# Scores of stage A as 64-row matmul pairs from one unpadded copy of the keys

## The chip, the cores and the metric

The kernel runs on one core of a Trainium2 chip. The metric is device time of one execution in microseconds (us), the median over several runs. The core has five engines that run side by side and meet at semaphores: PE (TensorE: matmuls, with weight loads, PEld, beside them), DVE (VectorE), ACT (ScalarE), POOL (GpSimd) and SP (SyncE, which here only issues DMAs). Each engine takes its own instructions strictly in the order in which the program has them, so an instruction that waits holds up all that stand behind it on that engine.

## What is computed

Two stages over 8 batches. Stage A is attention with a soft cap (12 heads, 448 tokens, 64 features per head); its output, with the heads put side by side as 768 features, is the input of stage B, a mixture of four attention experts with a causal mask and a top-2 gate.

```python
scores = scale * np.matmul(q, k.transpose(0, 1, 3, 2))
scores = cap * np.tanh(scores / cap)
attn = np.exp(scores)            # over the sum of its row
attn_out = np.matmul(attn, v)
...
x = attn_out, heads side by side
logits = x @ w_gate              # top 2 of 4 experts, softmax over the two
for e in range(E):
    q, k, v = x @ wq[e], x @ wk[e], x @ wv[e]
    a = causal softmax(scale * (q @ k.transpose(0, 2, 1)))
    out += gate[e] * (a @ v @ wo[e])
```

## The kernel before

Stage A works on pairs of heads, p = 0 to 47, six pairs to a batch. The loop over `prog` is the order of ACT: for each pair four tanh instructions `("T", p, 0..3)` and two exponentials `("E", p, 0..1)`, and, in two pairs of each batch, two exponentials of stage B, `("X", b, r, g)`, for the batch before. Each T or X reads a score tile in PSUM of 2 x 512 columns; there are two such tiles (`ps_score`, bufs=2), so the matmuls that fill one for the n-th read (`fill`, `b_fill`) can start when the read n-2 is over.

The path of one pair. SP loads q, k and v of two pairs at a time (`load`). POOL casts them to f16 (`a_cast`): q (L241), k (L242), the last 64 keys of both heads as two blocks on the diagonal of a 128x128 tile `ktz` (L245), then v. PE transposes q, `ktz` and k into one PSUM tile `tps` (`a_tr`, L272, L277, L279), and DVE copies that to SBUF: queries `qt` (L289, L293), the block-diagonal tail keys `kt` (L296) and the main keys, each head by itself, to `kk = kz[p % 4]` (L295, L297; the copies show as L223, the line of the helper `evac`). In `qt` the two heads lie one above the other, 64 rows each. In `kz` each head has its own columns, with zeros in the rows of the other head, so that a matmul over all 128 rows gives the scores of one head. `HALF` says which (head, block of 128 keys) are in each of the four score tiles: seven matmuls of 128 rows by 448 columns for a pair (L312), of which the tail block serves both heads at once. After tanh (L323) and exponential (L330), `a_pv_mm` multiplies with v (L351) and with the tail of v (`vtz`, L346), `a_pv_out` divides by the sums on DVE, and `a_xt` transposes the result into `xT` (L379, L390).

Stage B of a batch follows while stage A of the next batch runs. For each pair r of experts it has the projections q and k (`b_qk`, six matmuls each, L469), v and the gate's logits (`b_v`, L407), scores (`b_fill`, L522, L528), exponential (L540), a causal mask by POOL (L548), `b_pv` (L570), `b_ot` and `b_wo` (L594), copies to `ob` by DVE (L223), and the stores. Its weights are loaded by POOL, which issues up to three DMAs of the list `loads` in each `slot(p)` (L746), behind the casts of that slot.

What sets the order of PE: a planner, `Plan`, run in Python when the kernel is built. It keeps clocks of PE, DVE and ACT, and a list of work units with a PE time, a DVE time, dependences and a due time. Before each fill `do_fill` lets the planner put in as many units as fit ahead of the time at which ACT will need the fill (`plan.pump(rel, at - cost - 0.4)`), where `cost` is the PE time that the fill is taken to need. So a number in `do_fill` decides where the units of stage B stand between the fills. The planner takes no account of the DMAs of the weights: the first units of stage B depend on `x` (the transposed output of stage A) alone. At the end `last_batch` does stage B of batch 7 by itself; the units of batch 6 that are left by then are put in between.

```python
cost = 0.43 if o[0] == "X" else 0.38 if o[2] < 3 else 0.19
...
plan.pump(rel, at - cost - 0.4)
...
plan.parts(("q", b, r), 3, 1.13, 0.55, [x], t - 4.0, b_qk, b, r, "q")
```

Of the kernel before, what the change touches and what calls it, by code (L numbers as in the profile page):

```python
# [8 lines left out]
f32 = mybir.dt.float32  # L9
# [116 lines left out]
def kernel(  # L126
# [87 lines left out]
    nc.vector.memset(warm, 0.0)  # L214
    ident = const.tile([128, 128], f16, name="ident")
    make_identity(nc, ident)
    kz = [const.tile([128, 2, KM], f16, name=f"kz{i}") for i in range(4)]
    ktz = [const.tile([128, 128], f16, name=f"ktz{i}") for i in range(6)]
    for t in (ktz[0], kz[0], ktz[1], kz[1]):
        nc.vector.memset(t, 0.0)  # L220

    def evac(dst, src, act=False):
        (nc.scalar.copy if act else nc.vector.tensor_copy)(dst, src)  # L223
# [5 lines left out]
    def a_cast(p, eng=None):  # L229
        if p >= NP:  # L230
            return
        eng = nc.gpsimd if eng is None else eng
        if 2 <= p < len(ktz):
            nc.gpsimd.memset(ktz[p], 0.0)
        if 2 <= p < len(kz):
            nc.gpsimd.memset(kz[p], 0.0)
        assert p < 8 or ("pv", p - 8, 1) in plan.done and ("tr", p - 6) in plan.done
        qf, kf, vf, ktf, vtf = staged.pop(p)
        q16 = hd.tile([QP, QC, 2, Dh], f16, name=f"q16_{p}", tag="q16", bufs=6)
        k16 = hd.tile([128, KC, 2, Dh], f16, name=f"k16_{p}", tag="k16", bufs=6)  # L240
        eng.tensor_copy(q16, qf.rearrange("p h (c d) -> p c h d", c=QC))  # L241
        nc.gpsimd.tensor_copy(k16, kf.rearrange("p h (c d) -> p c h d", c=KC))  # L242
        for g in range(2):
            r = slice(64 * g, 64 * (g + 1))
            eng.tensor_copy(ktz[p % 6][r, r], ktf[r, :])  # L245
        cast[p] = (q16, k16)
        vcast[p] = (vf, vtf)
        if p > 1:
            a_castv(p)
# [16 lines left out]

    def a_tr(p):
        q16, k16 = cast.pop(p)
        assert p < 4 or (p - 4) not in qkt
        tps = ps_aux.tile([128, 1024], f16, name=f"tps_{p}", tag="aux")  # L270
        for c in range(QC):
            nc.tensor.transpose(  # L272
                tps[:, c * QP : (c + 1) * QP],
                q16[:, c, :, :].rearrange("p h d -> p (h d)"),
                ident[0:QP, 0:QP],
            )
        nc.tensor.transpose(tps[:, S : S + 128], ktz[p % 6], ident)  # L277
        for c in range(KC):
            nc.tensor.transpose(  # L279
                tps[:, S + 128 * (c + 1) : S + 128 * (c + 2)],  # L280
                k16[:, c, :, :].rearrange("p h d -> p (h d)"),
                ident,
            )


        qt = hd.tile([128, S], f16, name=f"qt_{p}", tag="qt", bufs=4)
        kt = hd.tile([128, 128], f16, name=f"kt_{p}", tag="kt", bufs=4)
        m = tps[:, 0:S].rearrange("m (c p) -> m c p", c=QC)
        nc.vector.tensor_copy(  # L289
            qt[:, 0:KM].rearrange("m (n c t) -> m n c t", n=3, c=QC),  # L290
            m[:, :, 0:96].rearrange("m c (n t) -> m n c t", t=32),
        )
        nc.vector.tensor_copy(qt[:, KM:S].rearrange("m (c t) -> m c t", c=QC), m[:, :, 96:QP])  # L293
        kk = kz[p % 4]
        evac(kk[0:64, 0, :], tps[0:64, S + 128 : S + 512], act=(p == 0))  # L295
        nc.vector.tensor_copy(kt, tps[:, S : S + 128])  # L296
        evac(kk[64:128, 1, :], tps[64:128, S + 128 : S + 512], act=(p == 0))  # L297
        qkt[p] = (qt, kk, kt)

    HALF = (((0, 0), (0, 1)), ((0, 2), (0, 3)), ((1, 0), (1, 1)), ((1, 2),))
    score = {}

    def fill(p, i):
        qt, kk, kt = qkt[p]
        if i == 3:
            del qkt[p]
        sc = ps_score.tile([128, 2, 512], f32, name=f"s{i}_{p}", tag="score")
        for o, (g, c) in enumerate(HALF[i]):  # L310
            lhsT = kt if c == KC else kk[:, g, 128 * c : 128 * (c + 1)]
            nc.tensor.matmul(sc[:, o, 0:S], lhsT, qt, start=True, stop=True)  # L312
        score[(p, i)] = sc

    y = {}
# [1 line left out]

    def tanh(p, i):
        g = i // 2
        n = len(HALF[i])  # L320
        if i % 2 == 0:
            y[(p, g)] = actp.tile([128, 4 - g, S], f16, name=f"y{g}_{p}", tag=f"y{g}")
        nc.scalar.activation(  # L323
            y[(p, g)][:, 2 * (i % 2) : 2 * (i % 2) + n, :], score.pop((p, i))[:, 0:n, 0:S],
            AF.Tanh, scale=isc / capf,
        )
# [7 lines left out]

    pvs = {}

    def a_pv_mm(p, i, n, heads):

        if n == 0 and 0 in heads:
            pvs[p, i] = ps_aux.tile([128, 2, 2, Dh + 1], f32, name=f"pv{i}_{p}", tag="aux")  # L340
        pv = pvs[p, i]
        w = WIN[2 * i + n]
        for g in heads:
            pt = pr[(p, g)]
            if g == 0:
                nc.tensor.matmul(  # L346
                    pv[:, n, :, :], pt[:, KC, w : w + 128], vtz[p % 8], start=(n == 0),
                    stop=False, skip_group_check=True,
                )
            for c in range(KC):  # L350
                nc.tensor.matmul(  # L351
                    pv[:, n, g, :], pt[:, c, w : w + 128], v16[p % 8][:, g, c, :],
                    start=False, stop=(c == KC - 1), skip_group_check=True,
                )

    def a_pv_out(p, i):
        pv = pvs.pop((p, i))
# [312 lines left out]
    def rows(w):  # L670
        return w.rearrange("(c p) m -> p c m", p=128)

    loads = [(wvg[:, :, E * Dh : E * Dh + E], rows(moe_w_gate))]
    for r in range(2):
        for e in (2 * r, 2 * r + 1):
            cols = slice(e % 2 * Dh, (e % 2 + 1) * Dh)
            loads += [(wq2[r][:, :, cols], rows(moe_wq[e])), (wk2[r][:, :, cols], rows(moe_wk[e]))]
        if r == 0:
            for e in range(E):
                loads += [(wvg[:, :, e * Dh : (e + 1) * Dh], rows(moe_wv[e]))]  # L680
    for e in range(E):
        loads += [(wo2[e // 2][e % 2 * Dh : (e % 2 + 1) * Dh, :], moe_wo[e])]


    EXPB = {HP * (b + 1) + 3 + 2 * r - (b == B - 2) * r: (b, r) for b in range(B - 1) for r in range(2)}
# [18 lines left out]
    def dur(o):  # L704
        if o[0] == "S":
            return 0.0
        if o[0] == "X":
            return 0.9
        return 0.06 + 0.373 * (4 - o[2] if o[0] == "E" else len(HALF[o[2]]))

    def fill_dep(o):
        return (("tr", o[1]),) if o[0] == "T" else (("q", o[1], o[2]), ("k", o[1], o[2]))
# [1 line left out]
    def do_fill():  # L714
        nonlocal nfill
        o = reads[nfill]
        rel = ends[nfill - 2] if nfill >= 2 else 0.0
        cost = 0.43 if o[0] == "X" else 0.38 if o[2] < 3 else 0.19
        for d in fill_dep(o):
            plan.force(d)  # L720
        at = plan.act + sum(dur(x) for x in prog[pos : where[nfill]])
        plan.pump(rel, at - cost - 0.4)
        plan.pe = max(plan.pe, rel, *(plan.done[d] for d in fill_dep(o))) + cost
        fill(*o[1:]) if o[0] == "T" else b_fill(*o[1:])
        plan.done[("f", nfill)] = plan.pe + plan.LAT
        nfill += 1
# [10 lines left out]
    def slot(p):  # L737
# [5 lines left out]
            plan.done[("cast", p + CAST)] = plan.act + 4.0  # L743
        for _ in range(3 if p else 1):
            if loads:
                nc.gpsimd.dma_start(*loads.pop(0))  # L746
        if p in (4, 5):
            b_const(p - 4)
        for i in (1, 2) if p == 0 else (p + TR,):
# [23 lines left out]
    def batch(b):  # L773
        x = ("xt", HP * b + HP - 1)
        t0, t1 = nom["X", b, 0, 0], nom["X", b, 1, 0]
        pace = 1.0 if b < B - 2 else 0.3
        for r, t in enumerate((t0, t1)):
            plan.parts(("q", b, r), 3, 1.13, 0.55, [x], t - 4.0, b_qk, b, r, "q")
            plan.parts(("k", b, r), 3, 1.13, 0.75, [x], t - 4.0, b_qk, b, r, "k")
        for n in range(4):  # L780
            d = [("v", b, n - 1)] if n else [x]
            plan.parts(("v", b, n), 2, 0.66, 0.6, d, t0 + 2.0 * n, b_v, b, n)
        plan.add(("g1", b), 0.0, 1.0, [("v", b, 3)], t1 + 1.0, b_gate, b, aux=None)
        plan.add(("g", b), 0.0, 0.8, [("g1", b), ("G", b)], t1 + 3.0, b_gate2, b, aux=None)
        for e in range(E):
            due = t1 + pace * (6.0 + 3.0 * e)
            d = [("X", b, e // 2, e % 2), ("g", b)] + [("pvB", b, e - 1)] * (e % 2)
            plan.add(("pvB", b, e), 0.46, 0.7, d, due, b_pv, b, e)
            if e % 2:
                plan.add(("oT", b, e // 2), 0.22, 0.35, [("pvB", b, e)], due, b_ot, b, e // 2)  # L790
        for n in range(4):
            for f in range(2):
                i = 2 * n + f
                d = [("oT", b, 1)] if i == 0 else [("wo", b, *divmod(i - 1, 2))]
                due = t1 + pace * (19.0 + 1.5 * i)
                plan.add(("wo", b, n, f), 0.33, 0.5, d, due, b_wo, b, n, f)

# [173 lines left out]
```

## Time and profile before

| what | us |
|---|---|
| median of 5 runs (339.12 to 341.41) | 340.76 |
| the profiled execution, its own time | 341.25 |
| its span, first to last instruction | 339.5 |
| ACT busy, 341 instructions | 308.4 |
| PE busy | 283.1 |
| DVE busy | 250.9 |
| POOL busy | 164.3 |
| tanh (L323), 192 instructions | 152.9 |
| exponential of stage A (L330), 96 instructions | 150.1 |
| score matmuls of stage A (L312), 336 instructions | 100.3 |

The span runs from the first to the last instruction; the time of an execution is 1.75 us longer. Busy times of several engines overlap. A matmul's record holds its way through the array too, so that records of matmuls that follow closely overlap: a lone matmul of 448 columns shows 0.35 us, while such matmuls in a row start every 0.19 us. The mean granted clock of TensorE is 0.975 of full speed. In a timeline each row has the start, the time to the end of the group, the engine, line and operation, the tiles (out<-in), the sizes, the number of instructions merged into the row, and in square brackets the idle time before it and what ended that.

### The profile page before, as it was taken

How to read it: one execution, taken by the hardware profiler on the slowest of the kernel's cores; microseconds unless marked ns; L12 is line 12 of the kernel's file. 1: busy time of each engine (PE TensorE's matmuls, PEld its weight loads, DVE VectorE, ACT ScalarE, POOL GpSimd, SP SyncE). 2: the span in 40 equal slices, each digit the busy share in tenths (PEclk: the TensorE clock that was granted, in tenths of full speed). 3: DMA queues.
4: the chain of work that ended last, by engine and by line, in shares of the span. 5: the costliest groups of instructions: out<-in, count | busy, mean ns of one | idle time of the engine just before them, and what ended most of it. 6: DMA issues, size and time to landing. Idle time of an engine off the chain costs nothing.

```text
span 339.5 us, 8954 instructions
## 1 busy us (share of the span) xinstructions
PE 283.1 (83%) x3295; PEld 192.1 (57%) x3295; DVE 250.9 (74%) x877; ACT 308.4 (91%) x341; POOL 164.3 (48%) x527
## 2 busy tenths in 40 slices
PE   4777668988899789997999779997999879979762
PEld 1354445655566556765676556765576657666441
DVE  2356646688668996789786997789796997787582
ACT  2989999999999999999999999999999999993612
POOL 2789999738507490538416580629325610220220
PEclk9779999999999999999999999999999999999797
DMA  6999999900354706590259307570441002110116
GB/s 160 266 311 248 261 248 238 249 2 3 128 173 126 227 4 215 163 274 4 82 177 287 110 2 235 181 238 2 138 151 42 3 2 93 48 26 2 46 58 223
DMA packets 65148, 46.21 MB, mean 136 GB/s; under 512 B 25872, under 2 KB 61584, under 8 KB 65104
## 3 DMA queue, kind: packets, MB, share of 16 engines
q1 hardware_dynamic: 53712, 43.43, 43.4%
q0 software_dynamic: 10512, 1.58, 6.5%
q10 hardware_dynamic: 880, 0.62, 0.7%
q8 instruction: 26, 0.43, 0.5%
q14 instruction: 18, 0.15, 0.1%
HBM read 36.19 MB, written 11.01 MB: 139 GB/s over the span
## 4 chain that ended last, share of the span: by engine, by line
ACT 82%; PE 4%; DMA 4%; POOL 3%; DVE 2%; issue 2%; SPq 1%; POOLq 0%; DVEq 0%
ACT y L323 38%; ACT p L330 36%; ACT pB L540 7%; DMA kf<-in_k_dram 1%; DMA ktf<-in_k_dram 1%; POOL pB L548 1%; PE qkps L469 1%; DMA out_dram<-ob 1%; PE vps L407 1%; DVE ob L223 1%; PE sB L528 1%; SPq L188 1%; PE pv L351 0%; POOL ktz L245 0%; PE wops L594 0%
## 5 line engine op out<-in xcount | busy, mean ns | idle before, releaser
L323 ACT ACTIVATE y<-s 128x896 f16<-128x896 f32 x192 | 152.9, 884 | 1.8 <-PE s L312 1.8
L330 ACT ACTIVATE p<-y 128x1792 f16<-128x1792 f16 x96 | 150.1, 1567 | 0.0
L548 POOL TENSOR_SCALAR_AFFINE_SELECT pB<-pB 128x128 f16<-128x128 f16 (+1 forms) x128 | 31.7, 277 | 140.7 <-ACT pB L540 139.6
L312 PE MATMUL s<-qt,kz 128*128 128x448 f16 x288 | 83.2, 361 | 14.8 <-ACT y L323 6.9
L351 PE MATMUL pv<-v,p 128*128 128x65 f16 x1152 | 66.7, 195 | 0.5 <-ACT p L330 0.3
L351 PEld LDWEIGHTS <-p 128*128 128x128 f16 x1152 | 54.4, 99 | 10.3 <-ACT p L330 1.2
L346 PE MATMUL pv<-vtz,p 128*128 128x130 f16 x192 | 42.3, 222 | 3.1 <-DVE kz L223 3.0
L364 DVE TENSOR_TENSOR xk<-pv,rc 128x256 f16<-128x256 f32 x96 | 40.8, 425 | 3.3
L312 PEld LDWEIGHTS <-kz 128*128 128x128 f16 x288 | 26.7, 98 | 27.6 <-issue 14.5
L223 DVE COPY ob<-wops 128x384 f32<-128x384 f32 (+1 forms) x60 | 33.1, 556 | 9.5 <-PE wops L594 8.6
L223 DVE COPY kz<-tps 64x384 f16<-64x384 f16 x94 | 32.9, 350 | 0.7
L540 ACT ACTIVATE pB<-sB 128x1024 f16<-128x1024 f32 (+1 forms) x32 | 31.8, 996 | 0.7 <-PE sB L528 0.5
L379 PE MATMUL xtp<-perm,xk 128*128 128x128 f16 x144 | 21.0, 223 | 13.2 <-DVE xk L364 13.0
L407 PE MATMUL vps<-wvg,xT 128*128 128x260 f16 (+1 forms) x192 | 31.5, 282 | 0.0
L594 PE MATMUL wops<-wo,oT 128*128 128x384 f16 x128 | 29.8, 325 | 1.7 <-DVE oT L588 1.7
L241 POOL CAST q<-qf 112x512 f16<-112x512 f32 x46 | 28.1, 611 | 2.8 <-DMA qf<-in_q_dram 0.8
L379 PEld LDWEIGHTS <-xk 128*128 128x128 f16 x192 | 14.6, 98 | 26.1 <-DVE xk L364 17.7
L363 DVE RECIPROCAL rc<-pv 128x4 f32<-128x4 f32 x96 | 17.2, 179 | 16.4 <-PE pv L351 15.1
L289 DVE COPY qt<-tps 128x384 f16<-128x384 f16 x48 | 17.0, 353 | 16.4 <-PE tps L279 16.1
L242 POOL CAST k<-kf 128x384 f16<-128x384 f32 x48 | 24.3, 507 | 5.0 <-DMA kf<-in_k_dram 5.0
L258 POOL CAST v<-vf 128x384 f16<-128x384 f32 x48 | 24.4, 508 | 3.4 <-DMA vf<-in_v_dram 0.4
L346 PEld LDWEIGHTS <-p 128*128 128x128 f16 x192 | 18.9, 98 | 12.5 <-DVE kz L223 3.7
(100 smaller groups left out, 499.8 us busy)
## 6 DMA issues: line engine op xcount, KB each, us to landing
qf<-in_q_dram SPq DMA_DIRECT2D x23, 448.0 KB, 5.0
out_dram<-ob SPq DMA_DIRECT2D x24, 384.0 KB, 2.8
kf<-in_k_dram SPq DMA_DIRECT2D x23, 384.0 KB, 5.3
vf<-in_v_dram SPq DMA_DIRECT2D x23, 384.0 KB, 5.1
ktf<-in_k_dram SPq DMA_DIRECT2D x46, 32.0 KB, 4.8
vtf<-in_v_dram SPq DMA_DIRECT2D x46, 32.0 KB, 4.3
out_dram<-ob SPq DMA_DIRECT2D x7, 192.0 KB, 2.9
qf<-in_q_dram ACTq DMA_DIRECT2D x2, 224.0 KB, 4.2
```

What stands on the lines that cost most here:

```text
L223: (nc.scalar.copy if act else nc.vector.tensor_copy)(dst, src)
L312: nc.tensor.matmul(sc[:, o, 0:S], lhsT, qt, start=True, stop=True)
L323: nc.scalar.activation(y[(p, g)][:, 2 * (i % 2) : 2 * (i % 2) + n, :], score.pop((p, i))[:, 0:n, 0:S], AF.Tanh, scale=isc / capf,)
L330: nc.scalar.activation(pt, y.pop((p, g)), AF.Exp, scale=capf)
L346: nc.tensor.matmul(pv[:, n, :, :], pt[:, KC, w : w + 128], vtz[p % 8], start=(n == 0), stop=False, skip_group_check=True,)
L351: nc.tensor.matmul(pv[:, n, g, :], pt[:, c, w : w + 128], v16[p % 8][:, g, c, :], start=False, stop=(c == KC - 1), skip_group_check=True,)
L364: nc.vector.tensor_tensor(xt[p][:, 2 * i : 2 * i + 2, :, :], pv[:, :, :, 0:Dh], rc.broadcast_to((128, 2, 2, Dh)), ALU.mult,)
L379: nc.tensor.transpose(ps[:, 128 * n : 128 * (n + 1)], src(n), first if n < 3 else last)
L407: nc.tensor.matmul(ps, xT[b][:, j, w : w + 128], wvg[:, j, 0:cols], start=(j == 0), stop=(j == NDC - 1),)
L540: nc.scalar.activation(pb[:, o0 : o0 + n], st[b].pop(("sc", r, g))[:, 0:n], AF.Exp, scale=isc)
L548: nc.gpsimd.affine_select(out=blk, in_=blk, compare_op=ALU.is_ge, fill=0.0, base=0, pattern=[[1, n]], channel_multiplier=-1,)
L594: nc.tensor.matmul(ps, st[b]["oT", r][:, w : w + 128], wo2[r][:, f * (D // 2) : (f + 1) * (D // 2)], start=(r == 0), stop=(r == 1),)
```

## The change

The keys of a pair are copied from `tps` to one tile `kt` of 128 x 512 by a single instruction; both heads lie one above the other in it, as in `qt`. The four `kz` tiles and their zeroing are gone. The score tile i (0 to 2) now holds key block i of both heads: two matmuls, one for each head, over 64 rows each (rows 0 to 63 and rows 64 to 127), which write the two halves (two PSUM banks) of the tile. The fourth is the tail block as before, over 128 rows. The sizes of the tanh and exponential instructions stay; what lies in `y` and `p` is in another order, and `a_pv_mm` takes it in that order, with the tail last.

The planner takes 0.25 us for every fill of stage A, where it took 0.38 us for the first three and 0.19 us for the fourth. The weights have names in `loads`, and the units of stage B that use them wait in the planner until 18 us of planned time after their DMA was put into the program.

```diff
-    kz = [const.tile([128, 2, KM], f16, name=f"kz{i}") for i in range(4)]
     ktz = [const.tile([128, 128], f16, name=f"ktz{i}") for i in range(6)]
-    for t in (ktz[0], kz[0], ktz[1], kz[1]):
+    for t in ktz[0:2]:
         nc.vector.memset(t, 0.0)
...
-        if 2 <= p < len(kz):
-            nc.gpsimd.memset(kz[p], 0.0)
...
-        kt = hd.tile([128, 128], f16, name=f"kt_{p}", tag="kt", bufs=4)
+        kt = hd.tile([128, 512], f16, name=f"kt_{p}", tag="kt", bufs=4)
...
-        kk = kz[p % 4]
-        evac(kk[0:64, 0, :], tps[0:64, S + 128 : S + 512], act=(p == 0))
-        nc.vector.tensor_copy(kt, tps[:, S : S + 128])
-        evac(kk[64:128, 1, :], tps[64:128, S + 128 : S + 512], act=(p == 0))
+        evac(kt, tps[:, S : S + 512], act=(p == 0))
...
-        for o, (g, c) in enumerate(HALF[i]):
-            lhsT = kt if c == KC else kk[:, g, 128 * c : 128 * (c + 1)]
-            nc.tensor.matmul(sc[:, o, 0:S], lhsT, qt, start=True, stop=True)
+        if i == KC:
+            nc.tensor.matmul(sc[:, 0, 0:S], kt[:, 0:128], qt, start=True, stop=True)
+        else:
+            for g in range(2):
+                r = slice(64 * g, 64 * (g + 1))
+                nc.tensor.matmul(
+                    sc[:, g, 0:S], kt[r, 128 * (i + 1) : 128 * (i + 2)], qt[r, :],
+                    start=True, stop=True,
+                )
...
-        for g in heads:
-            pt = pr[(p, g)]
-            if g == 0:
...
+        for h in parts:
+            pt = pr[(p, h)]
+            for c in (2 * h, 2 * h + 1):
+                if c == KC:
+                    nc.tensor.matmul(
+                        pv[:, n, :, :], pt[:, 2, w : w + 128], vtz[p % 8],
+                        start=False, stop=True, skip_group_check=True,
+                    )
+                    continue
+                for g in range(2):
+                    nc.tensor.matmul(
+                        pv[:, n, g, :], pt[:, 2 * (c % 2) + g, w : w + 128],
+                        v16[p % 8][:, g, c, :],
+                        start=(n == 0 and c == 0 and g == 0), stop=False, skip_group_check=True,
+                    )
...
-        cost = 0.43 if o[0] == "X" else 0.38 if o[2] < 3 else 0.19
+        cost = 0.43 if o[0] == "X" else 0.25
...
-                nc.gpsimd.dma_start(*loads.pop(0))
+                w, dst, src = loads.pop(0)
+                nc.gpsimd.dma_start(dst, src)
+                plan.done["w", w] = plan.act + 18.0
...
-            plan.parts(("q", b, r), 3, 1.13, 0.55, [x], t - 4.0, b_qk, b, r, "q")
-            plan.parts(("k", b, r), 3, 1.13, 0.75, [x], t - 4.0, b_qk, b, r, "k")
+            plan.parts(("q", b, r), 3, 1.13, 0.55, [x, ("w", ("q", r))], t - 4.0, b_qk, b, r, "q")
+            plan.parts(("k", b, r), 3, 1.13, 0.75, [x, ("w", ("k", r))], t - 4.0, b_qk, b, r, "k")
```

In the built programs PE has as many instructions before as after, DVE 877 before and 780 after. The units of PE stand in the same order up to the fills of pair 7, where stage B of batch 0 begins; from there on their order differs. With 0.38 and 0.19 put back in `do_fill`, the order of the units is that of before throughout; without the 18 us it is that of the changed kernel throughout.

More of the change, by code (lines that the diff above doesn't have):

```diff
@@ L268, in a_tr @@
         q16, k16 = cast.pop(p)
-        assert p < 4 or (p - 4) not in qkt
         tps = ps_aux.tile([128, 1024], f16, name=f"tps_{p}", tag="aux")
@@ L293, in a_tr @@
         nc.vector.tensor_copy(qt[:, KM:S].rearrange("m (c t) -> m c t", c=QC), m[:, :, 96:QP])
-        kk = kz[p % 4]
-        evac(kk[0:64, 0, :], tps[0:64, S + 128 : S + 512], act=(p == 0))
-        nc.vector.tensor_copy(kt, tps[:, S : S + 128])
-        evac(kk[64:128, 1, :], tps[64:128, S + 128 : S + 512], act=(p == 0))
-        qkt[p] = (qt, kk, kt)
-    HALF = (((0, 0), (0, 1)), ((0, 2), (0, 3)), ((1, 0), (1, 1)), ((1, 2),))
+        evac(kt, tps[:, S : S + 512], act=(p == 0))
+        qkt[p] = (qt, kt)
+    HALF = (2, 2, 2, 1)
     score = {}
     def fill(p, i):
-        qt, kk, kt = qkt[p]
-        if i == 3:
+        qt, kt = qkt[p]
+        sc = ps_score.tile([128, 2, 512], f32, name=f"s{i}_{p}", tag="score")
+        if i == KC:
             del qkt[p]
-        sc = ps_score.tile([128, 2, 512], f32, name=f"s{i}_{p}", tag="score")
-        for o, (g, c) in enumerate(HALF[i]):
-            lhsT = kt if c == KC else kk[:, g, 128 * c : 128 * (c + 1)]
-            nc.tensor.matmul(sc[:, o, 0:S], lhsT, qt, start=True, stop=True)
+            nc.tensor.matmul(sc[:, 0, 0:S], kt[:, 0:128], qt, start=True, stop=True)
[6 more added lines that the diff above has]
+                )
         score[(p, i)] = sc
@@ L319, in tanh @@
         g = i // 2
-        n = len(HALF[i])
+        n = HALF[i]
         if i % 2 == 0:
@@ L335, with a_pv_mm @@
     pvs = {}
-    def a_pv_mm(p, i, n, heads):
-        if n == 0 and 0 in heads:
+    def a_pv_mm(p, i, n, parts):
+        if n == 0 and 0 in parts:
             pvs[p, i] = ps_aux.tile([128, 2, 2, Dh + 1], f32, name=f"pv{i}_{p}", tag="aux")
@@ L342, in a_pv_mm @@
         w = WIN[2 * i + n]
-        for g in heads:
-            pt = pr[(p, g)]
-            if g == 0:
[L346 to L354, printed above, removed]
+        for h in parts:
[13 more added lines that the diff above has]
+                    )
     def a_pv_out(p, i):
@@ L671, in rows @@
         return w.rearrange("(c p) m -> p c m", p=128)
-    loads = [(wvg[:, :, E * Dh : E * Dh + E], rows(moe_w_gate))]
+    loads = [("v", wvg[:, :, E * Dh : E * Dh + E], rows(moe_w_gate))]
     for r in range(2):
@@ L676 @@
             cols = slice(e % 2 * Dh, (e % 2 + 1) * Dh)
-            loads += [(wq2[r][:, :, cols], rows(moe_wq[e])), (wk2[r][:, :, cols], rows(moe_wk[e]))]
+            loads += [(("q", r), wq2[r][:, :, cols], rows(moe_wq[e]))]
+            loads += [(("k", r), wk2[r][:, :, cols], rows(moe_wk[e]))]
         if r == 0:
             for e in range(E):
-                loads += [(wvg[:, :, e * Dh : (e + 1) * Dh], rows(moe_wv[e]))]
+                loads += [("v", wvg[:, :, e * Dh : (e + 1) * Dh], rows(moe_wv[e]))]
     for e in range(E):
-        loads += [(wo2[e // 2][e % 2 * Dh : (e % 2 + 1) * Dh, :], moe_wo[e])]
+        loads += [("o", wo2[e // 2][e % 2 * Dh : (e % 2 + 1) * Dh, :], moe_wo[e])]
     EXPB = {HP * (b + 1) + 3 + 2 * r - (b == B - 2) * r: (b, r) for b in range(B - 1) for r in range(2)}
@@ L708, in dur @@
             return 0.9
-        return 0.06 + 0.373 * (4 - o[2] if o[0] == "E" else len(HALF[o[2]]))
+        return 0.06 + 0.373 * (4 - o[2] if o[0] == "E" else HALF[o[2]])
     def fill_dep(o):
@@ L777, in batch @@
         for r, t in enumerate((t0, t1)):
-            plan.parts(("q", b, r), 3, 1.13, 0.55, [x], t - 4.0, b_qk, b, r, "q")
-            plan.parts(("k", b, r), 3, 1.13, 0.75, [x], t - 4.0, b_qk, b, r, "k")
+            plan.parts(("q", b, r), 3, 1.13, 0.55, [x, ("w", ("q", r))], t - 4.0, b_qk, b, r, "q")
+            plan.parts(("k", b, r), 3, 1.13, 0.75, [x, ("w", ("k", r))], t - 4.0, b_qk, b, r, "k")
         for n in range(4):
-            d = [("v", b, n - 1)] if n else [x]
+            d = [("v", b, n - 1)] if n else [x, ("w", "v")]
             plan.parts(("v", b, n), 2, 0.66, 0.6, d, t0 + 2.0 * n, b_v, b, n)
@@ L793, in batch @@
                 i = 2 * n + f
-                d = [("oT", b, 1)] if i == 0 else [("wo", b, *divmod(i - 1, 2))]
+                d = [("oT", b, 1), ("w", "o")] if i == 0 else [("wo", b, *divmod(i - 1, 2))]
                 due = t1 + pace * (19.0 + 1.5 * i)
```

## The prediction, as put on record

> **What bounds the kernel now.** I read the page first: busy times, then the chain of work that ended last.
>
> ```profile
> PE 283.1 (83%) x3295; PEld 192.1 (57%) x3295; DVE 250.9 (74%) x877; ACT 308.4 (91%) x341; POOL 164.3 (48%) x527
> ACT 82%; PE 4%; DMA 4%; POOL 3%; DVE 2%; issue 2%; SPq 1%; POOLq 0%; DVEq 0%
> ```
>
> ACT sets the time. Next the waits of ACT: for score tiles it waits 1.8 us in the whole run, three times, 1.3 us of it at once.
>
> ```profile
> ACT y L323 <- PE s L312: 1.8, 3, 1.3
> ```
>
> From 24.06 us to 308.6 us ACT works without a gap worth naming (windows 28 to 305 us: ACT busy in all of it). A faster PE gains nothing there. What can be won lies before 24 us and behind 308.6 us; what can be lost lies anywhere, as soon as a fill comes late. So I read the timeline at both ends, and then the order of PE in the changed program against the landings of DMAs.
>
> **The start.** The changed copies on ACT: two of 0.47 us, begun at 7.91 and 8.67, become one of 128x512. The rows of ACT copies from PSUM, 0.37 us at 256 columns, 0.47 at 384, 0.53 at 448, give 0.58. So the first fill starts 0.1 later than at 8.44. Its two matmuls took 0.37 each at the clock of that stretch (0.57 granted between 8 and 12 us): side by side they save 0.37, one after the other nothing. The first tanh (9.40) comes 0.27 earlier or 0.1 later. It matters little, for the wait that counts is at 22.7:
>
> ```profile
> 21.65 0.53 POOL L245 CAST ktz<-ktf 64x64 f16<-64x64 f32 x2
> 22.23 0.29 PE L277 MATMUL tps<-ident,ktz 128*128 128x128 f16 x1 [0.55 <-POOL ktz L245]
> 23.09 1.31 PE L312 MATMUL s<-qt,kz 128*128 128x448 f16 x3
> 24.06 1.35 ACT L323 ACTIVATE y<-s 128x896 f16<-128x896 f32 x2 [1.34 <-PE s L312]
> ```
>
> POOL's cast for pair 4 is late, PE waits in its transposes, the fill for T(2,2) stands behind them, and ACT is idle for 1.34. The change removes two zeroings of `kz` from POOL, 0.75 each. The first (11.17) stood ahead of a wait for the DMA of q that ends at 12.73 anyway: nothing. Behind the second (16.35) POOL works without a pause up to this cast: all that follows is 0.75 earlier. The fill saves up to 0.37 more at the slow clock. T(2,2) moves from 24.06 to 22.94 (23.31 if the two matmuls run one after the other): **-1.1, between -0.75 and -1.8** (the last if ACT's own end, earlier by 0.45, sets it). The removed zeroings on DVE (0.38 each, up to 2.16) stand ahead of a wait of 2.56 for q: nothing.
>
> **The middle, if the order were the same.** Per pair DVE has two copies of 0.35 and one of 0.21 less, and one of 128x512 more, about 0.44 by the copy of 448 columns (0.39). About 22 us less in all, off the path. PE: three fills of 2 x 0.19 become 0.19 each if the halves run side by side, 0.38 if not; no row here has a 64-row matmul. What passing from 128 to 64 rows and back costs is not in the trace either; bounds are nothing and the 0.16 by which a lone matmul (0.35) is longer than its step (0.19), paid twice. A fill then costs 0.19 to 0.71, against 0.38. I take 0.25, as the operands lie in separate rows and write separate banks. Hidden under ACT up to 0.63 (below).
>
> By the Trainium skill, "TensorEngine Tiling (Array Packing)", Key Properties, changing the tiling mode drains the TensorE, though tiles of one mode run independently; with two drains a fill would cost 0.19 + 0.33 = 0.52, still hidden, so the sum by it is the same, with less room.
>
> **The order.** The planner, told that fills are cheap, puts stage B in earlier. I followed the built order through batch 0, where weights have only just been loaded. In the changed kernel the first matmul of q of the second expert pair (`qps` of r=1) stands right behind the last fill of pair 8 and three matmuls of `vps`, ahead of the fill for T(9,0). It waits for two DMAs of `wq`. The second is issued by POOL as late as 45.96 and takes 14.5 to land:
>
> ```profile
> 45.96 0.84 POOL L746 DMA_DIRECT2D wq<-in_moe_wq_dram  x1
> wq<-in_moe_wq_dram POOLq DMA_DIRECT2D x1, 96.0 KB, 14.5
> ...
> 56.91 0.35 PE L312 MATMUL s<-qt,kz 128*128 128x448 f16 x1
> 57.10 0.49 PE L407 MATMUL vps<-wvg,xT 128*128 128x260 f16 x3
> ...
> 60.56 1.94 ACT L323 ACTIVATE y<-s 128x896 f16<-128x896 f32 x2
> 62.44 0.54 PE L469 MATMUL qps<-xT,wq 128*128 128x448 f16 x2
> ```
>
> Landing: 60.46. Before, that matmul came at 62.44, 2 us after it, and T(9,0) began at 60.56. Now PE arrives at 56.91 + 0.19 + 0.33 - 1.1 = 56.3; the landing, with POOL 0.75 earlier, is at 59.7. PE stands for 3.4 us. Queued behind it: 2 `qps`, 4 transposes, 3 `vps`, 2 `qps`, then the fill that ACT needs. At full clock 0.38 + 0.25 + 0.33 + 0.38 + 0.19 and 0.21 to ACT: T(9,0) at 61.4. The 18 us in the planner don't help: added to the planned time of slot 4 (7.9 + 4 x 5.6 = 30.3) they give 48.
>
> After gaps of 2.4, 1.1 and 1.5 us PE ran slowly here (8.4 to 11.5, 15.1 to 18.7, 22.3 to 25.2; 448 columns at 0.37):
>
> ```profile
> 16.00:20.00 4.00, 3.84 (x42) 2.82 (x39) 2.19 (x10) 4.00 (x5) 3.60 (x13) 0.67 1.06 307
> 20.00:24.00 4.00, 2.14 (x18) 1.51 (x19) 1.92 (x9) 2.72 (x3) 3.28 (x14) 0.75 1.08 309
> ```
>
> The last number but two is the granted clock. Some gaps of 1.3 us later on leave it at 1.00; this one is longer than all of these, so I take the slow clock: 0.75 + 0.45 + 0.65 + 0.75 + 0.37 + 0.21 = 3.2, T(9,0) at 62.9. **+2.3 against before (+0.85 at full clock)**; the gain of the start is used up in this and doesn't count again.
>
> The Trainium skill, "TensorE: Matmul & The Clock Gate", HAM oscillation, has a rule of no PE idle gaps above about 3.4 us; this gap is on that edge, so by the rule either end of the two could come, and the rows above choose the slow one.
>
> Behind T(9,0) stand 7 `pv`, a fill, 7 `pv`, 3 `vps`, 2 `qps`, 3 `vps` and the fill for X(0,0,0): 0.25 + 0.19 + 0.25 + 0.33 + 0.38 + 0.33 + 0.43 = 2.2 and 0.2 to ACT, while two tanh take 1.61 after 0.2: **+0.5** (0 to 0.8). Later batches have all weights. The closest place I found there is `pvB` of expert 2, now one fill behind X(b,1,0) with POOL's mask (1.27) between: POOL is idle there for 5 us before it, and T3 is 0.2 to spare: 0, at worst 0.3 in each of six batches.
>
> **The end.** Behind the last exponential (308.6) PE works without a gap to 314.8. Three matmuls of `qkps` (0.19 each) have moved ahead of that point and one `wops` unit (0.33) behind it: -0.25. After 323 two of the six `wops` units of batch 6 are gone from the end, so that DVE has two copies of 0.55 less ahead of `oT`:
>
> ```profile
> 328.97 2.08 DVE L223 COPY ob<-wops 128x384 f32<-128x384 f32 x4
> 331.08 0.39 DVE L588 COPY oT<-otp 128x448 f16<-128x448 f16 x1
> 332.07 1.02 DVE L223 COPY ob<-wops 128x384 f32<-128x384 f32 x2 [0.59 <-PE wops L594]
> 333.30 1.25 DVE L223 COPY ob<-wops 128x384 f32<-128x384 f32 x2 [0.20 <-DMA out_dram<-ob]
> ```
>
> `oT` comes 1.04 earlier, but the last copy needs the buffer whose store starts at 330.0 and takes 3.17: it moves from 333.99 to 333.3, -0.7. Together **-0.95** (-0.3 to -1.5).
>
> **Sum**: 2.3 + 0.5 - 0.95 = +1.85. The profiled execution, span 339.5 and 341.25 with what lies around it, becomes 343.1; it lies 0.5 above the median, so I forecast 340.76 + 1.85 = **342.6**. With the full clock and the other ends, +0.2 to +3.2: 341.0 to 344.0.
>
> **Rivals.**
> *No wait at the weights* (the landing comes 3 us sooner with the lighter start, or PE arrives late): then the start's -1.1 and the end's -0.95 remain, 338.7: faster. For it: landings of these loads range from 6 to 16 us. Against: all from 40 us on took 10 or more.
> *PE becomes the bound* (64-row matmuls one after the other, with two drains). Six pairs and the rest of a batch take ACT 37.4; PE is idle for 7.2 of 60 us between 140 and 200, so 4.5 in a batch of 18 such fills. It decides from 0.38 + 4.5/18 = 0.63 for a fill; at 0.71 it costs 0.08 x 18 x 7 = 10, so 342 to 351, say 346. That would also mean that the change doesn't do what it says.
> *The clock falls in pairs 3 to 7*: PE is busy for 58 to 77% of 28 to 52 us at clock 1.00, and less so after the change. If it goes slow there, waits of 0.3 to 0.5 a pair add about 2: 344.5. Against: slow work fills PE again.
>
> **Chances.** Forecast 0.58 (half a per cent, 1.7 us, is what a measurement can tell from no change: 0.36 of it slower, 0.22 same); no wait 0.22 (0.14 faster, 0.08 same); PE bound 0.12, all slower; clock 0.08 (0.06 slower, 0.02 same). Faster 0.14, same 0.32, slower 0.54. Range 338.9 to 345.2: a tenth lies above, in the PE rival, and less than that below.
>
> **What would show it.** In the profile after: ACT's longest wait for a score tile at about 59.5 to 63, with PE idle before the first `qps` of r=1 behind a DMA of `wq`; T(2,2) near 23; the fills at half their PE time; ACT busy still 308 with no other wait above 0.5. I am wrong if ACT waits for fills throughout (PE bound), or not at all. The last `oT` copy behind two copies of `ob` on DVE, not four, confirms the end.

## The result, and the profile after

The changed kernel took 342.88 us (median of 47 runs, 336.95 to 349.23), the kernel before on the same chips 339.73 (89 runs, 338.11 to 343.22). The ratio is 0.9998 with a 95% interval of 0.9983 to 1.0014: no change. That ratio leaves out executions more than 1.5% above the fastest of the same kernel, which for the changed kernel are 28 of 48 (the 47 runs and the profiled execution), all above 342.0; with all of them counted its mean is 0.9% above that of before. So its wide spread has to be understood before the ratio can be. The profiled execution has a span of 339.9 and took 341.57, against 339.5 and 341.25.

From the page of the changed kernel, the busy times, the clock in 40 slices and the chain of work that ended last:

```profile
PE 280.0 (82%) x3295; PEld 180.0 (53%) x3295; DVE 228.4 (67%) x780; ACT 308.0 (91%) x340; POOL 163.0 (48%) x525
PEclk9995879799999999999999999999999999999998
ACT 73%; POOL 8%; PE 7%; issue 4%; DMA 3%; DVE 3%; SPq 1%; POOLq 0%; ACTq 0%
```

ACT still has 308 us of work, DVE has lost 22.5. The chain now runs on ACT for 73% in place of 82, with POOL at 8 (3 before), PE at 7 (4) and issue at 4 (2); one of its pieces, start and length first, is this:

```profile
56.70 2.90 issue
```

Ahead of it the chain lies largely off ACT, behind it on ACT. The waits of ACT say where (waiting and releasing instruction; us in all, times, the longest):

```profile
ACT y L321 <- PE s L307: 3.7, 3, 2.6
ACT pB L541 <- PE sB L529: 0.9, 1, 0.9
```

Before, ACT waited 1.8 us for score tiles, 1.3 at once. The longest wait is now 2.6; ACT's timeline puts it at the fill for T(9,0):

```profile
57.97 1.86 ACT L328 ACTIVATE p<-y 128x1792 f16<-128x1792 f16 x1
62.44 1.96 ACT L321 ACTIVATE y<-s 128x896 f16<-128x896 f32 x2 [2.61 <-PE s L307]
65.33 1.02 ACT L541 ACTIVATE pB<-sB 128x1024 f16<-128x1024 f32 x1 [0.93 <-PE sB L529]
```

PE's timeline shows what PE did meanwhile:

```profile
56.01 0.35 PE L303 MATMUL s<-qt,kt 128*128 128x448 f16 x1
56.20 0.50 PE L408 MATMUL vps<-wvg,xT 128*128 128x260 f16 x3
59.60 0.54 PE L470 MATMUL qps<-xT,wq 128*128 128x448 f16 x2 [2.90 <-issue]
...
60.96 0.95 PE L470 MATMUL qps<-xT,wq 128*128 128x448 f16 x2
61.85 0.55 PE L307 MATMUL s<-qt,kt 64*128 64x448 f16 x2
```

PE stands still for 2.90 us ahead of the first `qps` of r=1, as forecast. The releaser reads "issue": the row names nothing, but the second `wq` load tells it. POOL's timeline has its issue, the view of DMAs its landing:

```profile
45.01 0.84 POOL L749 DMA_DIRECT2D wq<-in_moe_wq_dram  x1
```

```profile
wq<-in_moe_wq_dram POOLq DMA_DIRECT2D x1, 96.0 KB, 14.5
```

45.01 + 14.5 = 59.51, and PE goes on at 59.60. The pairs of matmuls before and behind (60.96: 0.95 for two of 448 columns, where 59.60 has 0.54) show the half clock that follows: 0.57 between 60 and 64 us.

The last exponential of stage A ends at 311.43 (308.60 before): 2.83 lost up to there. From it to the end of the span it is 28.5 us (30.9 before): 2.43 won there. ACT's timelines, before and after, have that last exponential in these rows:

```profile
304.42 4.18 ACT L330 ACTIVATE p<-y 128x1344 f16<-128x1344 f16 x3
```

```profile
307.25 4.18 ACT L328 ACTIVATE p<-y 128x1344 f16<-128x1344 f16 x3
```

In this execution the two nearly cancel: the span is 0.4 longer.

### The profile page after: what moved, and what is told of

The parts are those of the page before. It is cut to its first block, busy times and chain, and to the rows that moved or that the text cites. A ratio compares the mean times of both kernels' runs of the same rounds, so it can differ in the third digit from the quotient of the medians.

```text
span 339.9 us, 8882 instructions
## 1 busy us (share of the span) xinstructions
PE 280.0 (82%) x3295; PEld 180.0 (53%) x3295; DVE 228.4 (67%) x780; ACT 308.0 (91%) x340; POOL 163.0 (48%) x525
## 4 chain that ended last, share of the span: by engine, by line
ACT 73%; POOL 8%; PE 7%; issue 4%; DMA 3%; DVE 3%; SPq 1%; POOLq 0%; ACTq 0%
ACT p L328 33%; ACT y L321 32%; ACT pB L541 7%; DMA kf<-in_k_dram 1%; PE vps L408 1%; POOL q L238 1%; DMA ktf<-in_k_dram 1%; POOL wvg L749 1%; POOL ktz L242 1%; PE qkps L470 1%; PE qps L470 1%; POOL k L239 1%; POOL vtz L260 1%; DMA out_dram<-ob 1%; POOL wq L749 1%
## 5 line engine op out<-in xcount | busy, mean ns | idle before, releaser
L351 PE MATMUL pv<-v,p 128*128 128x65 f16 x1152 | 69.1, 197 | 3.1 <-ACT p L328 2.6
L351 PEld LDWEIGHTS <-p 128*128 128x128 f16 x1152 | 56.9, 100 | 26.6 <-issue 10.7
L307 PE MATMUL s<-qt,kt 64*128 64x448 f16 x288 | 53.2, 378 | 17.4 <-ACT y L321 11.5
L222 DVE COPY ob<-wops 128x384 f32<-128x384 f32 (+1 forms) x60 | 33.1, 556 | 12.2 <-PE wops L595 11.8
L307 PEld LDWEIGHTS <-kt 64*128 64x128 f16 x288 | 17.7, 94 | 41.8 <-issue 29.7
L595 PE MATMUL wops<-wo,oT 128*128 128x384 f16 x128 | 30.1, 326 | 1.3 <-DVE oT L589 1.3
L470 PE MATMUL qps<-xT,wq 128*128 128x448 f16 x84 | 23.1, 358 | 2.9 <-issue 2.9
L391 DVE COPY xT<-xtp 128x448 f16<-128x448 f16 x48 | 18.6, 387 | 8.6 <-PE xtp L380 7.9
L260 POOL CAST vtz<-vtf 64x64 f16<-64x64 f32 x96 | 22.5, 234 | 2.9
L470 PE MATMUL kps<-xT,wk 128*128 128x448 f16 x84 | 22.8, 353 | 0.1
```

Source lines behind the costliest of these rows:

```text
L307: nc.tensor.matmul(sc[:, g, 0:S], kt[r, 128 * (i + 1) : 128 * (i + 2)], qt[r, :], start=True, stop=True,)
L351: nc.tensor.matmul(pv[:, n, g, :], pt[:, 2 * (c % 2) + g, w : w + 128], v16[p % 8][:, g, c, :], start=(n == 0 and c == 0 and g == 0), stop ...
L470: nc.tensor.matmul(ps, w2[r][:, j, :], xT[b][:, j, :], start=(j == 0), stop=(j == NDC - 1), skip_group_check=(b == B - 1),)
```

## The experiments

Besides the time, four readings of each profile are used: the end of the last exponential of stage A ("E end"), the rest of the span behind it ("tail"), the granted clock in it, and ACT's waits before 100 us. Ratios are against the kernel before on the same chip.

| run | median us (runs; range) | ratio | E end | tail | lower clock of 316 to 320 and 320 to 324 |
|---|---|---|---|---|---|
| before | 339.73 (89; 338.11 to 343.22) | | 308.60 | 30.9 | 0.70 |
| after | 342.88 (47; 336.95 to 349.23) | 0.9998 | 311.43 | 28.5 | 1.00 |
| x1_again | 346.56 (6; 345.48 to 347.45) | 1.0164 | 317.34 | 28.4 | 1.00 |
| x2_w30 | 339.60 (12; 337.81 to 341.94) | 0.9969 | 308.94 | 28.5 | 1.00 |
| x3_cost38 | 341.79 (12; 340.71 to 344.70) | 1.0044 | 308.73 | 31.4 | 0.65 |
| x4_before_cost25 | 343.55 (7; 343.08 to 345.77) | 1.0092 | 313.40 | 28.4 | 1.00 |
| x5_loads_early | 342.33 (11; 339.39 to 352.9) | 1.0048 | 311.58 | 28.4 | 1.00 |
| x6_before25_w30 | 340.37 (12; 338.91 to 341.33, and one of 676.68) | 0.9998 | 309.64 | 28.4 | 1.00 |
| x7_same_rows | 343.23 (1 run) | | 311.37 | 30.1 | 0.68 |
| x8_w30_again | 339.34 (12; 337.98 to 341.79) | 0.9977 | 307.84 | 30.2 | 0.73 |
| x9_no_wait | 340.04 (12; 338.20 to 340.59) | 0.9982 | 308.19 | 30.1 | 0.70 |
| x10_after_third | 341.72 (12; 339.27 to 347.56) | 1.0025 | 309.74 | 28.4 | 1.00 |

**The changed kernel again (x1).** No edit.

> The changed kernel once more, for its spread and a second profile. Theory W (weights): PE stands before the first q of the second expert pair until a DMA of wq lands (59.5 us in the profile at hand), ACT loses 2.6 + 0.9 us there in every execution, and what differs between executions is when that DMA lands. Theory C (clock): the loss of the longer executions is made elsewhere, by a PE at half clock in pairs 3 to 8 and later. W expects in this profile one long wait of ACT, at about 60 us, with T(9,0) later in a longer execution by as much as the time is longer; C expects further waits of ACT for score tiles, above 1 us in sum, at other places.

Ratio 1.0164 [1.0127, 1.0201]. PE's timeline, and ACT's behind it:

```profile
56.34 0.50 PE L408 MATMUL vps<-wvg,xT 128*128 128x260 f16 x3
61.73 0.91 PE L470 MATMUL qps<-xT,wq 128*128 128x448 f16 x2 [4.89 <-issue]
```

```profile
64.99 0.92 ACT L321 ACTIVATE y<-s 128x896 f16<-128x896 f32 x1 [5.02 <-PE s L307]
```

The same program, the same place, a longer wait: the load is issued at 45.17 and lands 16.5 later, at 61.67, PE goes on at 61.73, and ACT loses 5.02 where it lost 2.61. A second loss stands at 84.30 (2.27 for `sB`), in a stretch at half clock that is shown below. So each theory holds a part: T(9,0) comes 2.55 later than in the first profile of the changed kernel, as W has it, but the time is 5.88 longer, and 2.27 of that is a loss elsewhere, as C has it. The other five runs of x1 have no profile.

**The weights held back longer (x2).** The order of PE changes: no `qps` of r=1 stands ahead of T(9,0) any more.

```diff
-                plan.done["w", w] = plan.act + 18.0
+                plan.done["w", w] = plan.act + 30.0
```

> The changed kernel with 30 us in place of 18 in the planner, which puts the first q of the second expert pair behind the scores of stage B, where it stood before the change. Theory W: no wait before T(9,0), which begins at about 59.5 (60.56 before the change, less 1.1 of the start); median 2.5 to 4 us below the changed kernel, 337 to 339, and a spread as narrow as that of the kernel before (5 us, not 12). Theory C: the spread stays wide and the median gains 1 us at most.

0.9969 [0.9939, 1.0000]; ACT's waits for score tiles are 2.1 in all, none at 62. The median is 7.0 below that of x1 on the same chip, and the spread 4.1 us. Taking the unit out of the way takes the loss away. The median lies above the 337 to 339 that was expected; in its profile the start's gain is lost to waits of 0.81 at 23.36 and 0.68 at 29.80.

**The order of before with the new tiles (x3).**

```diff
-        cost = 0.43 if o[0] == "X" else 0.25
+        cost = 0.43 if o[0] == "X" else 0.38 if o[2] < 3 else 0.19
```

> The changed kernel with the fill costs of before (0.38 and 0.19) in the planner: the order of units is that of before, only the tiles, the copies and the zeroings differ. Theory W: first q of the second expert pair at about 61.5, no wait; gain of the start alone, 0.75 to 1.1 us below the kernel before, 338.5 to 339; spread as before. Theory C: wide spread, as PE idles more in this kernel than in the changed one.

1.0044 [1.0016, 1.0073]: no wait at 62 either, but not faster: 341.79, where 338.5 to 339 was expected. The profiled execution has given the start back, at half clock (0.50 from 24 to 32 us), in ACT's timeline:

```profile
29.52 1.55 ACT L321 ACTIVATE y<-s 128x896 f16<-128x896 f32 x2 [1.31 <-PE s L307]
```

and has the longest tail of all, 31.4.

**The order of after with the old tiles (x4).** On the kernel before, nothing but the planner's number:

```diff
-        cost = 0.43 if o[0] == "X" else 0.38 if o[2] < 3 else 0.19
+        cost = 0.43 if o[0] == "X" else 0.25
```

> The kernel before with 0.25 in the planner for each fill, nothing else: 128-row matmuls in the order of the changed kernel. Theory W: PE waits for the landing at 60.4, T(9,0) at 62.5 to 63.8, ACT 2 to 3.5 us later than before from there on, 0 to 2.5 us of it won back at the end; median 340.5 to 343 with a spread as wide as that of the changed kernel. Theory C (the half-width matmuls leave PE too idle): narrow spread and no more than 1 us above before.

1.0092 [1.0057, 1.0127]. PE stands for 3.01 ahead of the same `qps` (60.86), and ACT waits at T(9,0):

```profile
62.75 1.73 ACT L323 ACTIVATE y<-s 128x896 f16<-128x896 f32 x2 [1.84 <-PE s L312]
```

So a loss comes with the order alone, without the 64-row tiles. It need not be the whole of the loss: x1 on the same chip is 3.0 slower than x4 by the median. Two things are not as theory W had them. The runs lie within 2.7 us, so the spread is not wide. And the clock did not fall behind the stand of 3.01, as the windows show:

```profile
60.00:64.00 4.00, 3.14 (x34) 2.25 (x35) 1.17 (x5) 2.16 (x3) 2.30 (x7) 1.00 1.09 230
```

(Here and below the columns are the window, its length, busy time and instructions of PE, PEld, DVE, ACT and POOL, the granted clock, the DMA share and GB/s.) It fell later, to 0.58 from 76 to 80 us, behind a stand of 1.97 for `xk`, and ACT lost 1.95 more at 80.35 for `sB`.

**The loads issued sooner (x5).**

```diff
-        for _ in range(3 if p else 1):
+        for _ in range(3):
```

> The changed kernel with three weight loads in slot 0 in place of one, so that every later load is put in two places sooner; the order of PE is untouched. Theory W (the wait for wq costs the time): the second wq is issued some 4 us sooner (about 41) and lands at 55 to 58; PE waits less than 1.5 us there, T(9,0) begins at 59.5 to 61; POOL's 1.7 us in slot 0 may cost ACT up to 1.2 near 28 us. Time 338 to 341, clearly under the changed kernel beside it. If the loads only share one slow stream and land as late as before (theory Q, the stream is full), T(9,0) stays at 62 or later and the time at that of the changed kernel.

1.0048 [1.0021, 1.0075]. The second `wq` is issued at 43.56, 1.45 sooner than in the changed kernel's profile, takes 17.6 and lands at 61.16, 1.65 later; PE waits 1.75 for it. An earlier issue did not bring an earlier landing: 55 to 58 was expected by theory W, and T(9,0) begins at 63.02, as theory Q has it. But that start isn't a clean sign for Q, since ACT itself was late by then and waits only 0.43 there. The loads moved into slot 0 also held up POOL's casts: ACT waits 2.77 at 31.21.

**The old tiles with the better order (x6).** The kernel before with the planner's 0.25, the names in `loads`, and 30 us for 18.

> The kernel before (128-row matmuls, padded keys) with 0.25 us for each fill and the 30 us wait in the planner: the very order of units of the run with 30 us, without the half-width tiles. If the tiles themselves are worth anything (theory H), it is 1 us or more slower than that run. If only the order counts and the tiles' gain is hidden under ACT (theory O), it is the same within 0.7 us, 338.5 to 340; the start should lose 0.75 to 1.2 for the zeroing on POOL.

0.9998 [0.9973, 1.0023], 340.37, beside 339.34 for the new tiles in the same order on the same chip (x8, below). The tiles, with the lighter start, are worth 0.7 by the ratios and 1.0 by the medians, but the intervals overlap. In the profiles the start explains that much: T(4,0) begins at 32.61 in x6 and at 31.59 in x8. What made one run of x6 take 676.68 and one of x5 352.9 is not known.

**Both halves on the same rows (x7).** This leaves out the scores of the second head; the size of each instruction stays.

```diff
-                    sc[:, g, 0:S], kt[r, 128 * (i + 1) : 128 * (i + 2)], qt[r, :],
+                    sc[:, g, 0:S], kt[0:64, 128 * (i + 1) : 128 * (i + 2)], qt[0:64, :],
```

> The changed kernel with both matmuls of a fill on rows 0 to 63 (the scores of the second head are left out, those of the first are computed twice), for the price of a fill alone. If the two halves run side by side only because they lie on different rows, a fill takes 0.19 more here than the 0.30 from one start to the next group's that the changed kernel shows at full clock: 0.49. If they already ran one after the other, nothing changes: 0.30.

A fill at full clock in PE's timeline, of x7 and then of the changed kernel:

```profile
56.51 0.55 PE L307 MATMUL s<-qt,kt 64*128 64x448 f16 x2
56.99 0.36 PE L351 MATMUL pv<-v,p 128*128 128x65 f16 x6
```

```profile
55.04 0.36 PE L307 MATMUL s<-qt,kt 64*128 64x448 f16 x2
55.34 0.35 PE L351 MATMUL pv<-v,p 128*128 128x65 f16 x6
```

From the start of the fill to the next group it is 0.48 on the same rows and 0.30 on two halves, against 0.37 for two matmuls of 128 rows (58.93 to 59.30 in the kernel before). The halves do run side by side: 0.18 less, one step of 448 columns. And 0.30 is 0.11 above that step of 0.19; the same 0.11 stands between 0.48 and 0.37, where nothing runs side by side. So I take 0.11 as what going to 64 rows and back costs here.

**x2 once more (x8).** The same kernel on another chip.

> The run with 30 us once more, for its interval beside the others on one chip: ratio to before 0.993 to 0.998, ACT without a wait for a score tile between 32 us and the last exponential.

0.9977 [0.9950, 1.0005], 339.34: the gain repeats, at the edge of what twelve runs can tell.

**The order of after without the wait (x9).** The q of the second expert pair in batch 0 is computed from the weights of the first, which have long landed; those q are left out of the result.

```diff
-                ps, w2[r][:, j, :], xT[b][:, j, :], start=(j == 0), stop=(j == NDC - 1),
+                ps, w2[0 if b == 0 and which == "q" else r][:, j, :], xT[b][:, j, :],
+                start=(j == 0), stop=(j == NDC - 1),
```

> The changed kernel, in the same order on PE, with the q of the second expert pair of batch 0 computed from the weights of the first pair, which have long landed (so the q of experts 2 and 3 of batch 0 are left out). Nothing else differs, so this is the changed kernel without the wait. Theory W: PE is not held at 56 us, T(9,0) begins at 59.2 to 60, the second wait at X(0,0,0) goes too; 3.5 us or more below the changed kernel beside it, 336 to 339 in nearly all executions, spread 5 us. Theory C (a PE too idle and at half clock makes the long executions): the median is within 1.5 us of the changed kernel and the spread as wide.

0.9982 [0.9957, 1.0007], and the spread shrinks to 2.4 us. `qps` runs at 57.30 straight behind `vps`, T(9,0) starts at 60.35 without a wait; PE's and ACT's timelines:

```profile
56.96 0.50 PE L408 MATMUL vps<-wvg,xT 128*128 128x260 f16 x3
57.30 0.54 PE L470 MATMUL qps<-xT,wq 128*128 128x448 f16 x2
```

```profile
60.35 1.86 ACT L321 ACTIVATE y<-s 128x896 f16<-128x896 f32 x2
```

The order itself costs nothing that these runs can tell; the wait inside it does. The gain over the changed kernel beside it (x10) is 1.7 us by the medians, not the 3.5 or more that theory W expected.

**The changed kernel beside x9 (x10).** No edit, the same chip as x9.

> The changed kernel a third time, beside the run without the wait. Theory W: the landing of the second wq, read from this profile, gives T(9,0) as landing + 2.9 us at half clock or + 1.9 at full clock, and the time follows: 341.6 for a landing at 59.5, about 2.5 us more for each 2 us later.

341.72, with 12 runs from 339.27 to 347.56, where the kernel before had 338.69 to 342.22; ratio 1.0025 [0.9993, 1.0057]. Its profiled execution drew a short wait:

```profile
56.84 0.50 PE L408 MATMUL vps<-wvg,xT 128*128 128x260 f16 x3
58.04 0.54 PE L470 MATMUL qps<-xT,wq 128*128 128x448 f16 x2 [0.70 <-issue]
```

The load was issued at 45.71 and landed 12.2 later, at 57.91; ACT loses nothing at T(9,0), which starts at 60.26.

Three profiles of one program thus give three prices for the same instruction:

| profile | issue + flight = landing | PE stands | ACT waits at T(9,0) | time |
|---|---|---|---|---|
| x10_after_third | 45.71 + 12.2 = 57.91 | 0.70 | 0 | 339.86 |
| after | 45.01 + 14.5 = 59.51 | 2.90 | 2.61 | 341.57 |
| x1_again | 45.17 + 16.5 = 61.67 | 4.89 | 5.02 | 347.45 |

The time follows the landing in these three, with other terms beside it: the first loses 1.22 at 76.82 in a stretch at half clock, and from the second row to the third a loss of that kind (2.27) and a longer wait for X (1.65 for 0.93) come on top. On one chip the spread is 8.3 us with the wait (x10) and 2.4 without it (x9): most of the changed kernel's spread comes with this wait.

## Why the prediction was wrong

The forecast was slower, at 342.6; the verdict is no change. The wait at the weights came where it was forecast, but its price was not one number, and the end was mis-sized. In the profiled execution alone the sum misses by the end: the order and X cost 2.81 where 2.8 was forecast, the end gave 2.43 where 0.95 was, and the span is 0.4 longer, not 1.85. Over the executions it misses because the order's price differs from one to the next. The range that the sum gives beside it, +0.2 to +3.2, does not follow from its terms either: their bounds add up to -0.65 and +2.8 (without the 0.3 in each of six batches).

**The start, -1.1: right in most profiles.** T(2,2) moved from 24.06 to 22.20, not 22.94; ACT's own end set it, and the move is 1.86, at the bound of 1.8 given for that:

```profile
22.20 1.39 ACT L321 ACTIVATE y<-s 128x896 f16<-128x896 f32 x2
...
28.44 1.56 ACT L321 ACTIVATE y<-s 128x896 f16<-128x896 f32 x2 [0.45 <-PE s L307]
```

Part is handed back at 28.44 (half clock): by T(4,0), at 31.48, 32.50 before, it is -1.02. This gain varies too. The three profiles with the start of before (before, x4, x6) have T(4,0) at 32.50 to 32.61; of the seven with the changed start (x5 and x7 alter it further), five have it at 31.48 to 31.78, but x3 has it at 32.56 and x2 at 32.84.

**The order, +2.3, and X, +0.5: the step that failed.** In the profiled execution T(9,0) came at 62.44 (62.9 forecast), later by 1.88 than before, and X(0,0,0) added 0.93, above its bound of 0.8: 2.81 for 2.8 forecast. PE stood for 2.90 (3.4 forecast), the landing was 59.51 (59.7), the clock behind it 0.57. So far it is as forecast. What failed is the sentence "the landing, with POOL 0.75 earlier, is at 59.7. PE stands for 3.4 us": one landing of one execution became the price, and the only doubt kept was that of the clock (+0.85 to +2.3). The runs show 0.70, 2.90 and 4.89 of standing for the same program, and times from 336.95 to 349.23. The slow clock behind the wait, 1.45 of the 2.3, is no fixed part of it either: T(9,0) came 2.84 behind the first `qps` in the changed kernel, at 0.57, and 1.89 behind it in x4, at 1.00, although PE had stood for 3.01 there. In the kernel before `qps` came 2 us behind the landing, which hid this draw. The rival "no wait at the weights" was counted as another world with a chance of 0.22; it is the lower end of the same draw. Of the executions that enter the ratio only the profiled one's landing is known, 59.51; that most of the others had earlier ones is likely, but not shown. The median of all 47, 342.88, lies 0.3 from the forecast. That is luck and no confirmation: it is 3.15 above the 339.73 of before, where 1.85 was forecast on a base of 340.76, and it mixes the wait with the mis-sized end.

**The end, -0.95: mis-sized, -2.43 in the profiled execution.** The lines of DVE that answer to those of before:

```profile
330.35 1.03 DVE L222 COPY ob<-wops 64x384 f32<-64x384 f32 x2
331.42 0.39 DVE L589 COPY oT<-otp 128x448 f16<-128x448 f16 x1
332.40 1.49 DVE L222 COPY ob<-wops 128x384 f32<-128x384 f32 x3 [0.59 <-PE wops L595]
334.09 0.56 DVE L222 COPY ob<-wops 64x384 f32<-64x384 f32 x1 [0.20 <-PE wops L595]
```

`oT` stands behind two copies of `ob`, as forecast. But the tail is not one number either. With the changed kernel's order there it is 30.1 or 30.2 in x7, x8 and x9, whose clock falls to 0.68 to 0.73, and 28.4 or 28.5 in the seven profiles in which it stays at 1.00; with the order of before it is 30.9 (0.70) and 31.4 (0.65, x3). At a like clock the order is worth 0.7 to 0.8 (the kernel before against x7, x8 and x9), near the 0.95 of the forecast; the other 1.6 to 1.7 are the clock. Windows of the kernel before and of the changed one:

```profile
316.00:320.00 4.00, 1.99 (x12) 1.30 (x13) 3.12 (x14) 2.96 (x6) 0.32 (x2) 0.87 0.07 27
320.00:324.00 4.00, 3.94 (x31) 2.83 (x30) 0.30 (x2) 3.15 (x5) 2.87 (x12) 0.70 0.00 0
```

```profile
316.00:320.00 4.00, 2.63 (x28) 1.60 (x27) 2.06 (x6) 1.49 (x4) 0.00 (x0) 1.00 0.50 197
320.00:324.00 4.00, 3.00 (x26) 2.29 (x27) 2.48 (x11) 3.05 (x6) 1.23 (x6) 1.00 0.00 0
```

and of x8, which has the end's order of after:

```profile
316.00:320.00 4.00, 2.62 (x16) 1.65 (x17) 2.65 (x12) 3.05 (x6) 0.95 (x4) 0.84 0.00 0
320.00:324.00 4.00, 3.89 (x37) 2.85 (x36) 0.84 (x4) 2.48 (x4) 2.67 (x12) 0.73 0.00 0
```

x2, the same program as x8, stayed at 1.00. So the clock there is a draw as well, and the order alone does not fix it. Whether the order shifts the odds is not shown: it was low in both profiles with the order of before and in three of the ten others. In all twelve PE stands for 1.37 or 1.38 and then for 0.99 or 1.00 us ahead of the stretch, whether the clock then falls or not.

**The tiles.** A fill was taken as 0.25 and measured 0.30; the bounds were 0.19 and 0.71. In all, the records of the first three fills fell from 83.2 to 53.2 us, and ACT's other waits stayed small: hidden, as forecast. The Trainium skill, "TensorEngine Tiling (Array Packing)", Key Properties, says that a change of the tiling mode drains the array; the 0.11 above one step agrees with drains, but short ones.

**The rivals.** PE did not become the bound. *The clock falls in pairs 3 to 7* came true beside the forecast (0.50 from 28 to 32 us and from 40 to 44, 1.00 before in both) but cost 0.45 there (1.31 in x3), not 2: most of the slow work was hidden under ACT.

**Where the gain is.** Without the wait the changed kernel is faster by 0.6 (x9), 1.1 (x2) and 0.8 us (x8), each from its ratio, not by the 2.05 of start and end together; the intervals touch or pass 1, and x9's median is 0.2 above that of before on its chip. Of what was run, the kernel of x2 and x8 is the version to keep: its median is 3.3 to 3.5 below that of the changed kernel, and below that of the kernel before by about 1, at the edge of the intervals.

**Open.** Why the landing differs by 4 us between executions, and why all six runs of x1 are long, was not tried. What makes the clock in the tail fall is not known. Why x3 is 0.4% slower rests on one profile (1.31 at 29.52 and the tail).

## What to carry to other kernels

When a change moves an instruction to within a few microseconds of a DMA's landing, the price can be a draw and not a number: read the flight times of all like transfers and let the range cover them before the order is judged. In a planner that knows PE times but no transfers, lowering the cost of one unit pulls every later unit forward, and the first one that reads fresh data will be found by it; a hold that covers the longest flight (30 us for 18 here) is cheap. And compare the spread of two kernels before their ratio, since a wait that comes and goes shows there first.

## What was not expected of the hardware

**Half clock after a gap of 1.4 us, but not always.** In the changed kernel, x1, x9 and x10 PE stands for 1.40 or 1.41 us behind DVE's `xk` at the same point of batch 0; in the changed kernel it is this row of the timeline:

```profile
74.89 0.23 PE L380 MATMUL xtp<-perm,xk 128*128 128x128 f16 x1 [1.41 <-DVE xk L365]
```

In the profiled execution of the changed kernel and in x9 the clock stays at 1.00; in x10 it is 0.57 in the next window, and in x1, in PE's timeline and the windows:

```profile
78.16 0.29 PE L380 MATMUL xtp<-perm,xk 128*128 128x128 f16 x1 [1.41 <-DVE xk L365]
```

```profile
76.00:80.00 4.00, 2.30 (x25) 1.56 (x25) 3.24 (x16) 4.00 (x5) 1.58 (x6) 0.72 0.00 0
80.00:84.00 4.00, 4.00 (x47) 3.13 (x46) 2.90 (x11) 2.00 (x3) 0.00 (x0) 0.50 0.00 0
```

PE is busy for all of 80 to 84 and ACT for half of it: the slow stretch costs ACT 2.27 at 84.30 (1.22 in x10). The Trainium skill, "TensorE: Matmul & The Clock Gate", HAM oscillation, puts the edge at idle gaps of about 3.4 us; here 2.90 was enough in the changed kernel, and 1.41 in x1, so the measurement decides against it as a safe limit for this kernel. Nor is there another limit in these rows: behind the 3.01 of x4 the clock stayed at 1.00.

**The flight of a 96 KB weight load.** The second `wq` load took 12.2 us (issued at 45.71), 14.5 (45.01), 16.5 (45.17) and, issued earliest (43.56), 17.6.
